# 66 narrow matmuls of ones in front, a bank of their own for the first state sums, and one routing step behind the last gate sums

## The chip, the core and the metric

The kernel runs on one core of one Trainium2 chip. The metric is device time in microseconds (us) of one execution; lower is better.

## The reference

A gated linear recurrence (4 batches, 8 heads, 768 steps, 48 channels a head) feeds a mixture of experts with two levels of routing (3072 tokens of 384 channels, 4 groups of 4 experts, 1024 hidden units). Cut to what matters:

```python
f = 1.0 / (1.0 + np.exp(-f_logit))
for t in range(S):
    state = f[:, :, t, :, None] * state + np.einsum('bhd,bhe->bhde', k[:, :, t], v[:, :, t])
    y[:, :, t] = np.einsum('bhd,bhde->bhe', q[:, :, t], state)
x = y.transpose(0, 2, 1, 3).reshape(B * S, H * D)
# each token: best group by x @ w_group, best expert in it by x @ w_expert[g]
h = np.maximum(x_of_expert @ w1[g, e], 0.0)
out[tokens] = (g_weight * e_weight)[:, None] * (h @ w2[g, e])
```

## The kernel before

**Two stages.** The first computes the recurrence in chunks of 128 steps and routes the tokens; the second gathers each expert's tokens and runs the two layers. The first stage is cut into 12 units: unit i is chunk c = i // 2 and the batch pair s = i % 2. Each unit goes through steps that have one-letter names: `c` bounds the gate logits (L597, VectorE); `g` takes Exp and Ln of them (L607, L610, ScalarE), sums the logarithms along time by a matmul with a triangle (`cs`, L616, TensorE) and takes Exp of the sums both ways (`eq` L617, `kh` L618); `m` multiplies q and k by them (L636, L639, VectorE); `t` turns both by TensorE transposes (`tr_q`, `tr_k`, L650) that ScalarE copies out (L651); `s` makes the scores (`ap`, L704 or L689) and masks them on VectorE (`am`, L707 or L692); `n` makes the chunk's state sums (`ds`, L721, TensorE) and on VectorE the next state (`st`, L726 to L729); `w` makes the outputs (`y`, L741 to L753), copied to `xT` by ScalarE (L756); `d` and `x` make the routing logits (`lT`, `lg`, L769, L774) and the rows of x (`x_ps`, L794) that are written to `x_dram`; `b` brings the chunk's decays (L659).

**Routing.** When both units of a chunk are done, a routing generator (`route`, L188) stands in a queue, and each step `r` takes it one yield further. For each chunk it ranks the tokens, writes weights and token numbers as `meta` into `x_dram` (L256, issued by GpSimd), and multiplies one-hot matrices `ln` and `val` (made by VectorE, L236, L243) into the slot table (`tb`, L261, TensorE; added by VectorE, L266). After the fourth chunk (`CLOSE`, c = 3) the two smallest experts are chosen, and GpSimd gathers their rows from `x_dram` (`xg`, L404). Those are turned on TensorE (`xg_ps`, L440) by step `e`, and their layers fill TensorE while the last routing runs.

**What sets the order.** TensorE, VectorE, ScalarE and SyncE run in exactly the order in which the program issues the work (`manual_schedule`, L85). That order is written by hand as strings of step names: `BEGIN` (L844) for the first three units, then `EVEN`, `ODD` or an entry of `ORDERS` (L850) for each later i; a name's number is the unit, in the later strings relative to i. GpSimd's order is left to the scheduler. In `BEGIN` the two steps `n0 n1` stand next to each other: the second step of unit 0 (VectorE makes its state, L729) and the first of unit 1 (TensorE makes its sums).

**PSUM.** Of the eight banks, seven belong to a pool from which `bank()` (L80) takes one for each product, the one that has been free longest. The eighth is the tile `ds` (L534), which holds the state sums of every unit. A tile whose reader has not finished makes the next writer wait; the program's semaphores see to that.

**The start.** SyncE issues the loads of the first units. Ahead of all other matmuls TensorE runs ten matmuls of ones in bf16 (`warm`, L892 to L894) whose product nobody reads: 128 rows, 128 weight columns, 512 columns that pass through. They wait only for VectorE's memset of `onesb` (L107).

Of the kernel before, what the change touches and what calls it, by code (L numbers as in the profile page):

```python
# [10 lines left out]
FP32 = mybir.dt.float32  # L11
# [7 lines left out]
P = 128  # L19
# [4 lines left out]
def kernel(  # L24
# [12 lines left out]
    nc = tc.nc  # L37
    B, H, S, D = q.shape
# [7 lines left out]
    HP = H // 2  # L46
    DP = 64
# [29 lines left out]
    def const(shape, dtype, name):  # L77
        return cp.tile(shape, dtype, tag=name, name=name)

    def bank(shape, name):  # L80
        return ps.tile(shape, FP32, tag="bank", name=name)
# [11 lines left out]
    onesb = const([P, P], BF16, "onesb")  # L93
# [305 lines left out]
    def fetch(pool, rows, n, top=N, late=False):  # L399

        w = {"n": n, "pool": pool, "early": top < N, "late": late, "blocks": [(j, min(P, n - j * P)) for j in range((n + P - 1) // P)]}
        w["x"] = pool.tile([P, len(w["blocks"]), RW], FP32, tag="xg", bufs=2 if pool is ep else 6, name="xg")
        for j, m in w["blocks"]:
            nc.gpsimd.indirect_dma_start(out=w["x"][:, j, :], out_offset=None, in_=x_dram[0:1 + top, :], in_offset=bass.IndirectOffsetOnAxis(ap=rows[:, j:j + 1], axis=0))  # L404
        return w
# [124 lines left out]
    with ExitStack() as fast:  # L530
        sb = fast.enter_context(tc.tile_pool(name="sb", bufs=2))
        fp = fast.enter_context(tc.tile_pool(name="fp", bufs=1))
        sums = fast.enter_context(tc.tile_pool(name="sums", bufs=1, space=bass.MemoryType.PSUM))
        ds = sums.tile([P, 2, HP, D], FP32, tag="ds", name="ds")  # L534

        def kept(shape, name):
            return fp.tile(shape, FP32, tag=name, name=name)
# [24 lines left out]
        NU = len(units)  # L562
# [21 lines left out]
        def load(i, names):  # L584
            c, s = units[i]
            w = live.setdefault(i, {"v": pads["v"][i % 4], "qh": pads["qh"][i % 3]})
            for nm in names:
                if nm not in w:
                    w[nm] = sb.tile([P, 2, H, D], FP32, tag="ld_" + nm, bufs=3 if nm == "f" else 2, name="ld_" + nm)
                for b in parts(i) if nm == "f" else (slice(0, 2),):  # L590
                    nc.sync.dma_start(out=heads(w[nm][:, b])[:, :, 0:D], in_=SRC[nm][2 * s + b.start:2 * s + b.stop, :, c * P:(c + 1) * P, :].rearrange("b h t d -> t (b h) d"))
# [118 lines left out]
        def stated(i):  # L710

            c, s = units[i]
            w = live[i]
            if c == NC - 1:
                return
            old, new = states[s][c % 2], states[s][(c + 1) % 2]
            wide = D if i else DP
            for a in range(HP):
                for b in range(2):
                    for r in range(2):  # L720
                        nc.tensor.matmul(ds[DP * r:DP * r + wide, b, a, :], lhsT=w["kh"][:, b, 2 * a + r, 0:wide], rhs=w["v"][:, b, 2 * a + r, 0:D], start=True, stop=True)  # L721
            yield
            dst = new[:, :, :, 0:D]
            gv = w["g"].unsqueeze(3).broadcast_to((P, 2, HP, D))
            if c:
                nc.vector.tensor_tensor(dst, old[:, :, :, 0:D], ds, OP.add)  # L726
                nc.vector.tensor_tensor(dst, dst, gv, OP.mult)
            else:
                nc.vector.tensor_tensor(dst, ds, gv, OP.mult)  # L729
            yield  # L730
# [103 lines left out]
        def advance(gens):  # L834
# [6 lines left out]


        STAGES = {"c": bounded, "g": gated, "m": multiplied, "t": turned, "z": crossed, "s": scored, "n": stated, "w": weighed, "d": done, "x": listed, "b": decayed}
        BEGIN = """c0 g0 p g0 g0 m0 m0 m0 m0 l2 t0 t0 t0 t0 h c1 g1 g1 s0 s0 s0 s0 g1 g1 p w0 w0 n0 m1 m1 m1 m1 l3 h x0 x0 x0  # L844
            t1 t1 t1 t1 b1 c2 g2 g2 s1 s1 s1 s1 p d0 g2 g2 n0 n1 w1 w1 m2 m2 l4 n1
# [4 lines left out]
        ORDERS = {  # L850
            NU - 4: "l+2 o d-2 n-1 r r r x-1 x-1 t t t t g+1 g+1 x-1 r z s s w s s c+2 d-1 g+2 w g+2 n m+1 m+1".split(),
            NU - 3: "l+2 o d-2 r r x-1 x-1 t t t t b n-1 r g+1 g+1 x-1 r s s s s c+2 w d-1 g+2 w g+2 n m+1 m+1 r n".split(),
            NU - 2: "d-2 r x-1 x-1 r t t t t r g+1 g+1 x-1 s s s s w d-1 w n m+1 m+1 k".split(),
            NU - 1: "d-2 r r n-1 x-1 x-1 t t t t r x-1 r s s s s w b d-1 w r r".split(),
            NU: "d-2 r e d-1 x-1 x-1 d-1 x-1 r r r e e r e r r e r r e r e r r e e e e e".split(),
        }
# [32 lines left out]
        load(1, ("qh", "k"))  # L889
        load(2, ("f",))  # L890
        load(1, ("v",))
        warm = bank([P, 4, P], "warm")  # L892
        for _ in range(10):
            nc.tensor.matmul(warm, lhsT=onesb, rhs=onesb.unsqueeze(1).broadcast_to((P, 4, P)), start=True, stop=True)  # L894
        for tok in BEGIN:
            step(tok[0], int(tok[1:] or 0))
        for i in range(BEGUN, NU + 1):
# [67 lines left out]
    for n in range(GE - 1):  # L965
        w = ws[n]
# [105 lines left out]
    with tc.If(more > 0), ExitStack() as late:  # L1072
# [5 lines left out]
        with tc.For_i(0, last, 1) as i:  # L1078
# [14 lines left out]
            w = fetch(ep, row, P, late=True)  # L1093
# [32 lines left out]
```

## Time and profile before

| | |
|---|---|
| time, median of 3 runs | 420.16 us (418.62 to 420.23) |
| the profiled execution's own time | 416.59 us |
| its span, first to last instruction | 414.8 us |
| TensorE: matmuls / weight loads, busy share | 97% / 89% |
| VectorE, ScalarE, GpSimd, busy share | 64%, 39%, 20% |
| HBM traffic over the span | 213 GB/s |
| first stage, about | 0 to 136 us |
| second stage, about | 136 us to the end |

How to read the views. In the timeline a line gives the start in us, the duration in us, the engine, the line of the program, the operation, output and input, partitions and elements, the count, and in brackets how long the engine had been idle and what ended that. PE is TensorE's matmuls, PEld its weight loads, which overlap them; DVE is VectorE, ACT ScalarE, POOL GpSimd, SP SyncE; a q behind a name is the engine's queue of DMA issues. A matmul's duration includes its way through the array, so consecutive matmuls overlap in the records: the distance between two starts says how long one occupies TensorE. fp32 matmuls are recorded as two each. In the list of waits a line names who waited, for whom, the total in us, how often, and the longest. TensorE's own idle time is short beside its busy time; an engine that isn't the bottleneck can be idle at no cost.

### The profile page before, as it was taken

What the parts mean: (1) busy time and instruction counts of PE and PEld (TensorE: products, weight loads), DVE (VectorE), ACT (ScalarE), POOL (GpSimd) and SP (SyncE); (2) the same over time, 40 slices, a digit from 0 to 9 for tenths busy, and PEclk for the clock granted to TensorE, in tenths of its full rate; (3) what the DMA queues carried; (4) which work ended last, traced back from release to release, by engine and by line L of the source; (5) the groups of instructions that cost most, each with busy time, mean ns of one, the idle gap of its engine ahead of it and who ended that gap; (6) DMA issues with size and microseconds to landing.
All of it is one profiled execution on the core that took longest, in us unless ns stands there. A gap on an engine that the chain in (4) does not pass through costs nothing.

```text
span 414.8 us, 10271 instructions
## 1 busy us (share of the span) xinstructions
PE 403.0 (97%) x4143; PEld 371.1 (89%) x4143; DVE 264.6 (64%) x780; ACT 162.7 (39%) x365; POOL 84.4 (20%) x132
## 2 busy tenths in 40 slices
PE   8989999999999999999999999999999999999994
PEld 3878878888878978989999999999999999999992
DVE  6666787778898722630899768486595595584230
ACT  6767878788555412211213122222232232232220
POOL 5000010101012157001042221311311230120230
PEclk9999999999999999999999999999999999999999
DMA  9999886869999459974829468586496596585010
GB/s 191 200 223 206 174 162 135 159 139 263 262 358 346 148 184 338 394 273 180 292 70 334 149 231 275 156 314 224 156 350 184 203 344 198 185 318 163 28 47 24
DMA packets 132146, 88.99 MB, mean 215 GB/s; under 512 B 102582, under 2 KB 122748, under 8 KB 132090
## 3 DMA queue, kind: packets, MB, share of 16 engines
q1 hardware_dynamic: 125666, 75.50, 61.2%
q0 software_dynamic: 5792, 11.92, 9.5%
q10 hardware_dynamic: 632, 0.83, 0.6%
q8 instruction: 35, 0.57, 0.5%
q14 instruction: 21, 0.17, 0.1%
HBM read 78.71 MB, written 9.83 MB: 213 GB/s over the span
## 4 chain that ended last, share of the span: by engine, by line
PE 47%; issue 30%; DMA 8%; POOL 6%; DVE 5%; ACT 2%; POOLq 1%; DVEq 0%
PE hp L450 12%; DMA out_dram<-yt,xg 7%; PE yo L486 7%; PE yo L471 4%; POOL out_dram L461 4%; PE cs L616 3%; POOL xg L404 2%; PE y L753 2%; PE ap L689 2%; PE x_ps L794 2%; PE tr_k L650 2%; DMA xg<-x_dram,rows_e 2%; PE tr_q L650 2%; PE y L745 2%; PE y L741 2%
## 5 line engine op out<-in xcount | busy, mean ns | idle before, releaser
L450 PE MATMUL hp<-xe,w 128*128 128x128 f32 (+14 forms) x864 | 138.6, 320 | 0.0
L450 PEld LDWEIGHTS hp<-xe,w 128*128 128x128 f32 x864 | 135.8, 190 | 0.8
L486 PE MATMUL yo<-h,w 128*128 128x230 f32 (+13 forms) x672 | 115.8, 333 | 0.0
L433 DVE STREAM_TRANSPOSE yr<-yT 32x192 f32<-32x192 f32 (+1 forms) x208 | 70.5, 339 | 70.4 <-ACT yT L487 67.8
L486 PEld LDWEIGHTS yo<-h,w 128*128 128x128 f32 x672 | 113.7, 190 | 0.2
L426 DVE STREAM_TRANSPOSE xe<-xg 32x192 f32<-32x192 f32 (+1 forms) x208 | 69.7, 335 | 8.6 <-PE hp L450 5.6
L451 ACT ACTIVATE h<-hp 128x256 f32<-128x256 f32 (+14 forms) x72 | 34.4, 478 | 103.5 <-PE hp L450 103.5
L461 POOL DMA_INDIRECT out_dram<-yt,xg x32 | 34.5, 1078 | 148.1 <-ACT yt L458 142.5
L487 ACT COPY yT<-yo 128x230 f32<-128x230 f32 (+13 forms) x42 | 13.5, 326 | 80.5 <-PE yo L486 80.5
L404 POOL DMA_INDIRECT xg<-x_dram,rows_p x30 | 29.6, 987 | 53.7 <-DMA out_dram<-yt,xg 25.4
L471 PE MATMUL yo<-w,h 128*128 128x384 f32 x64 | 21.3, 486 | 0.0
L707 DVE TENSOR_TENSOR am<-ap,tri 128x512 f32<-128x512 f32 x24 | 14.9, 681 | 8.5 <-PE ap L704 8.5
L616 PE MATMUL cs<-ld_f,tri 128*128 128x384 f32 x48 | 19.0, 521 | 0.0
L471 PEld LDWEIGHTS yo<-w,h 128*128 128x128 f32 x64 | 11.9, 190 | 7.4
L623 POOL DMA_DIRECT2D ends<-eq x10 | 5.4, 541 | 55.0 <-ACT eq L617 55.0
L458 ACT ACTIVATE yt<-yr,xg 128x384 f32<-128x384 f32 (+13 forms) x26 | 14.4, 604 | 5.4 <-DVE yr L433 5.4
L756 ACT COPY xT<-y 128x512 f32<-128x512 f32 x24 | 13.4, 587 | 7.5 <-PE y L745 5.4
L692 DVE TENSOR_TENSOR am<-ap,seen 128x384 f32<-128x384 f32 x24 | 12.2, 552 | 5.8 <-PE ap L689 5.8
L650 PE MATMUL tr_q<-ident,qh 128*128 128x128 f32 x96 | 14.5, 273 | 0.7 <-issue 0.6
L651 ACT COPY Tk<-tr_k 128x512 f32<-128x512 f32 x24 | 15.0, 629 | 0.0
L651 ACT COPY Tq<-tr_q 128x512 f32<-128x512 f32 x24 | 14.8, 618 | 0.4 <-PE tr_q L650 0.4
L617 ACT ACTIVATE eq<-cs 128x384 f32<-128x384 f32 x24 | 12.4, 518 | 5.2 <-PE cs L616 5.0
(187 smaller groups left out, 438.0 us busy)
## 6 DMA issues: line engine op xcount, KB each, us to landing
w<-in_moe_w_dram SPq DMA_DIRECT2D x34, 1536.0 KB, 8.4
qh<-in_q_dram SPq DMA_DIRECT2D x12, 384.0 KB, 4.7
ld_k<-in_k_dram SPq DMA_DIRECT2D x12, 384.0 KB, 4.0
v<-in_v_dram SPq DMA_DIRECT2D x12, 384.0 KB, 5.5
ld_f<-in_f_logit_dram SPq DMA_DIRECT2D x11, 384.0 KB, 5.5
x_dram<-x_kept SPq DMA_DIRECT2D x2, 1536.0 KB, 9.4
x_dram<-x POOLq DMA_DIRECT2D x2, 384.0 KB, 7.1
x_dram<-x ACTq DMA_DIRECT2D x2, 384.0 KB, 6.1
```

What stands on the lines that cost most here:

```text
L404: nc.gpsimd.indirect_dma_start(out=w["x"][:, j, :], out_offset=None, in_=x_dram[0:1 + top, :], in_offset=bass.IndirectOffsetOnAxis(ap=rows ...
L426: squares(w, lambda n, k_, rk, g, rg: nc.vector.transpose(out=xT[rg, 0:n, k_], in_=x[rk, 0:n, g]))
L433: squares(w, lambda n, k_, rk, g, rg: nc.vector.transpose(out=y[rk, 0:n, g], in_=yT[rg, 0:n, k_]))
L450: nc.tensor.matmul(hp[:, o, :], lhsT=w1[:, ko, (f + o) * P:(f + o + 1) * P], rhs=w["xT"][:, ko, :], start=(ko == 0), stop=(ko == KO - 1))
L451: nc.scalar.activation(h[:, f:f + 2, :], hp, AF.Relu)
L461: sent = nc.gpsimd.indirect_dma_start(out=out, out_offset=bass.IndirectOffsetOnAxis(ap=w["x"][0:m, j, DM + 1:RW].bitcast(U32), axis=0), in ...
L471: nc.tensor.matmul(yp, lhsT=w["h"][:, fo, :], rhs=w2[:, fo, :], start=(fo == 0), stop=(fo == FO - 1))
L486: nc.tensor.matmul(yp, lhsT=w2[:, fo, m * P:(m + 1) * P], rhs=w["h"][:, fo, :], start=(fo == 0), stop=(fo == FO - 1))
L616: nc.tensor.matmul(cs.rearrange("t h d -> t (h d)"), lhsT=tri, rhs=nl[:, b], start=True, stop=True)
L650: nc.tensor.transpose(out=pt[:, a, :], in_=w[nm + "h"][:, b, 2 * a:2 * a + 2, :].rearrange("t r d -> t (r d)"), identity=ident)
L651: nc.scalar.copy(w["T" + nm][:, b], pt)
L707: nc.vector.tensor_tensor(am[:, r], ap[r], tri.unsqueeze(1).broadcast_to((P, HP, P)), OP.mult)
```

## The change

Three edits. The warm-up becomes 66 matmuls of 128 columns in place of ten of 512. The state sums of unit 0 go to a bank of the pool, and the tile of the eighth bank (now called `later`) holds those of the units after it; units 0 and 1 (not only unit 0) use 64 weight columns a head, so that the whole of either bank is written. In the string for i = 10 (`NU - 2`) one `r` moves from ahead of `g+1 g+1` to behind it: on TensorE the `tb` matmuls of the fourth chunk follow the `cs` matmuls of unit 11 instead of going ahead of them.

```diff
-        ds = sums.tile([P, 2, HP, D], FP32, tag="ds", name="ds")
+        later = sums.tile([P, 2, HP, D], FP32, tag="ds", name="ds")
...
             old, new = states[s][c % 2], states[s][(c + 1) % 2]
-            wide = D if i else DP
+            wide = D if i > 1 else DP
+            ds = later if i else bank([P, 2, HP, D], "ds")
             for a in range(HP):
...
-            NU - 2: "d-2 r x-1 x-1 r t t t t r g+1 g+1 x-1 s s s s w d-1 w n m+1 m+1 k".split(),
+            NU - 2: "d-2 r x-1 x-1 r t t t t g+1 g+1 r x-1 s s s s w d-1 w n m+1 m+1 k".split(),
...
-        warm = bank([P, 4, P], "warm")
-        for _ in range(10):
-            nc.tensor.matmul(warm, lhsT=onesb, rhs=onesb.unsqueeze(1).broadcast_to((P, 4, P)), start=True, stop=True)
+        warm = bank([P, 1, P], "warm")
+        for _ in range(66):
+            nc.tensor.matmul(warm, lhsT=onesb, rhs=onesb.unsqueeze(1).broadcast_to((P, 1, P)), start=True, stop=True)
```

The orders of VectorE, ScalarE, GpSimd and SyncE are the same in both programs; on TensorE the order differs only in these places. From unit 0's sums on, the pool hands out its banks in another rotation.

## The prediction

> **What bounds the kernel now.** I read the page first, then TensorE's waits, then the timeline of the three places that the change touches, then who waits for what follows them. TensorE (PE) sets the pace:
>
> ```profile
> PE 403.0 (97%) x4143; PEld 371.1 (89%) x4143; DVE 264.6 (64%) x780; ACT 162.7 (39%) x365; POOL 84.4 (20%) x132
> ...
> PEclk9999999999999999999999999999999999999999
> ```
>
> PE is busy almost throughout, so a stall taken out of its queue should come off the end, unless a later stall takes it back. The waits of PE are few; four of them matter here (engine, line, what it waited for, total us, times, longest):
>
> ```profile
> PE ds L721 <- DVE st L729: 1.2, 1, 1.2
> PE warm L894 <- DVE onesb L107: 1.0, 1, 1.0
> PE tb L261 <- DVE val L243: 0.8, 1, 0.8
> PE xg_ps L440 <- DMA xg<-x_dram,rows_e: 0.7, 1, 0.7
> ```
>
> The change touches the first three. The fourth comes after all of them, and will matter. The timeline of the start (start us, us):
>
> ```profile
> 1.04 4.45 PE L894 MATMUL warm<-onesb 128*128 128x512 bf16 x10 [1.04 <-DVE onesb L107]
> ...
> 5.35 2.25 PE L616 MATMUL cs<-ld_f,tri 128*128 128x384 f32 x4
> ...
> 5.84 0.52 ACT L610 ACTIVATE ld_f<-ld_f 128x384 f32<-128x384 f32 x1
> ...
> 6.99 0.49 ACT L617 ACTIVATE eq<-cs 128x384 f32<-128x384 f32 x1 [0.62 <-PE cs L616]
> ...
> 8.75 1.02 DVE L639 SCALAR_TENSOR_TENSOR kh<-kh,ld_k 128x384 f32<-128x384 f32 x2
> ...
> 11.44 1.98 PE L704 MATMUL ap<-Tq,Tk 48*64 48x128 f32 x64
> ```
>
> The ten warm matmuls end just as the first sums (cs) can begin. Behind cs lies a chain without slack: eq on ACT, the products qh and kh on DVE back to back until 9.77, the turning of kh and the gates on PE, then ap. What moves cs moves all of it. The line of cs gives min/median/max ns:
>
> ```profile
> L616 PE MATMUL cs<-ld_f,tri x48: 486/486/979, 5.3 to 118.6; 128*128 128x384 f32 x48
> ```
>
> The 979 ns is the very first, at 5.35; the fourth, at 7.11, takes 486. The first two records occupy PE from 5.35 to 6.76 (0.70 each), the third from 6.76 to 7.11 (0.36). So PE ran at half speed until about 6.76, although the PEclk row shows nines from the start: that row can't be used here. The warm loads fit: their starts are 0.425 us apart for 512 columns, 0.106 per 128.
>
> **What the Trainium skill says.** "TensorE: Matmul & The Clock Gate", Part 1: a cold TensorE runs at half clock and is released after a sustained busy window of about 3.4 us, and the window is free-running, so the moment varies between executions. The trace agrees as far as it goes: PE began at 1.04 and was released near 6.76, 5.7 us later, between one window and two. The same page, "Back-to-back issue gap": 128 columns cost N/1.2 ns cold (107; the trace's 106) and N/2.4 + 2.5 ns warm (56; no row shows bf16 at 128 columns warm). "PSUM — Partial Sum Buffer", section on bank collisions: a writer and a reader of one bank must be kept apart by semaphores. That is the ds wait of 1.2 us: PE may not write unit 1's state sums while DVE has yet to read unit 0's from the same bank.
>
> **Part 1, 66 warm matmuls of 128 columns.** Removed: 10 x 0.425 = 4.25 us of PE. Added: 66, at 0.106 until the release and about 0.055 after. With the release at 6.76: (6.76 - 1.04) / 0.106 = 54 cold ones, and 12 x 0.055 = 0.66, end 7.42. cs then starts at 7.42 instead of 5.35, but warm: its first result is there at 7.42 + 0.36 + 0.49 = 8.27 instead of 6.95, +1.3 us for the whole chain. The release is free-running, so I bound it. At 4.45 (one window after 1.04): 32 cold, 34 x 0.055, end 6.3, first cs at 7.2. The old kernel, released then too, would gain 0.4 against its profile (ACT's second Ln ends at 6.36 and DVE's memsets at 7.33, so not more): the difference is 0.2 + 0.4 = +0.6. At 7.86 (two windows): end 8.0, first cs 8.8, +1.9; the old one then runs its second cs cold too and loses 0.7; difference +1.2. So +0.6 to +1.3; I take **+1.0**. No cover hides it: the old warm-up ended where its input arrived (Ln of the first half ends at 5.24), the new one outlasts that by 1 to 2.7 us.
>
> **Part 2, another bank for unit 0's state sums.** PE and then DVE, from their timelines around it:
>
> ```profile
> 23.06 1.56 PE L616 MATMUL cs<-ld_f,tri 128*128 128x384 f32 x4
> 25.82 0.93 PE L721 MATMUL ds<-v,kh 128*48 128x48 f32 x32 [1.20 <-DVE st L729]
> 26.57 1.93 PE L745 MATMUL y<-am,v 128*64 128x128 f32 x32
> ```
>
> ```profile
> 25.21 0.55 DVE L729 TENSOR_TENSOR st<-ds,decays 128x384 f32<-128x384 f32 x1
> ```
>
> The sums of unit 1 wait for DVE's L729 at 25.21, which stands behind masks and constants in DVE's order. With a bank of their own they start when cs has left PE: 23.06 + 4 x 0.33 = 24.4 instead of 25.82, -1.4. Their inputs are old (kh from 17.7), and y behind them needs am, which DVE ends at 24.20. What is late next: the second xT copy on ACT, then x_ps and tr_q at about 28.2 instead of 29.68; qh is ready at 26.63, kh at 27.50, in time. The borrowed bank is held from 16.6 to 25.8, leaving six in the ring; I followed the new bank waits of the built program up to unit 2, and each is on a reader that ends before PE gets there (tr_k on gw copies, done 18.4; second cs on am, done 22.4). The 64 wide weights cost nothing: 16 matmuls of 48 columns, as before. Between 0 (if the ring bites) and -1.5; I take **-1.4**. The steps up to 98.9 us are a chain of PE work, so it is carried on; from there DVE and ACT lead, but started by PE's ap.
>
> **Part 3, tb behind the last cs.** PE:
>
> ```profile
> 117.43 0.29 PE L261 MATMUL tb<-val,ln 128*128 128x64 bf16 x4 [0.85 <-DVE val L243]
> 117.55 1.54 PE L616 MATMUL cs<-ld_f,tri 128*128 128x384 f32 x4
> 119.02 2.06 PE L704 MATMUL ap<-Tq,Tk 48*128 48x128 f32 x32
> ```
>
> cs needs only Ln of unit 11, done at 114.86, so it can run from 116.45, when tr_k leaves PE, to 117.9; val is ready at 117.37, so tb then waits for nothing, and ap starts at 118.05 instead of 119.02: -0.95 on PE. Behind tb in its new place is only ap. DVE reads tb at 118.62; tb's result is there at 118.2. DVE's, ACT's, POOL's and SP's orders don't change, nor any DMA's place. But PE's next stall, on POOL's chain, then PE's:
>
> ```profile
> 119.25 0.76 POOL L256 DMA_DIRECT2D x_dram<-meta  x1 [2.36 <-DVE number L304]
> 126.35 1.07 POOL L404 DMA_INDIRECT xg<-x_dram,rows_e  x1 [6.33 <-DVE best L204]
> ```
>
> ```profile
> 133.37 0.33 PE L774 MATMUL lg<-ident,lgT 128*128 128x128 f32 x1
> 134.38 0.52 PE L440 MATMUL xg_ps<-ident,xg 128*128 128x128 f32 x3 [0.68 <-DMA xg<-x_dram,rows_e]
> ```
>
> PE stands before xg_ps until the gather lands. The gather follows the meta write (issued 119.25, landing 6.2 us later), and that follows DVE's own queue, busy without a gap from 106 to 120. None of it comes earlier because PE does. So PE arrives 0.95 sooner and waits 0.95 longer. Bounds: 0 to -0.95; I take **-0.2**, for small things such as x rows sent earlier. Parts 1 and 2 are not swallowed so: they shift DVE's queue too.
>
> **Sum.** 1.0 - 1.4 - 0.2 = -0.6 on the profiled execution's 416.59 (span 414.8 and 1.8 around it): 416.0. The three timed runs have a median of 420.16, 3.6 above it; the same step on the median gives **419.6 us**.
>
> **Rivals.**
> (B) The timed runs lack the early release. They lie 2.0 and 3.6 us above the profiled one; one window late costs half of 3.4, 1.7, and two cost 3.4. If the input arrives late in them, PE has a gap between the warm matmuls and cs and the window fails. 66 cold matmuls last 7.0 us, over two windows, so they always contain a whole one. Then the new kernel runs as the good profile did, 416.0 plus up to 1: 416.8. For it: the steps of 2.0 and 1.6. Against: a gather of 7.9 us under weight loads can vary as much.
> (C) Slower: the loads of the warm matmuls don't hide. A cold load is 0.15 us in the trace; if a pair took 0.15 + 0.106 = 0.256, 22 would be done at 6.76 and the other 44 take 5.6, end 12.4, +6.3 for cs: 6.3 - 1.6 = +4.7, 424.9. In general the end is at 3.9 + 33 x the cold pair's time; from 0.115 us the gains are eaten, from 0.18 it is slower by over 0.5%. Against: tb's four pairs of 64 columns start 0.03 us apart, so loads hide there.
> (D) The ds gain doesn't reach the end (a ring or DMA wait before 98.9): 420.16 + 1.0 = 421.2.
>
> **Chances.** A (forecast) 0.47, 418.5 to 420.6; B 0.31; D 0.14; C 0.08. A measurement of this kernel can tell about 0.5%, 2.1 us, from no change. Faster by more: B and a little of A, 0.34. Slower by more: C and the top of D, 0.11. Same: 0.55. The range runs from inside B to the top of D, 416.4 to 421.7.
>
> **What would show it.** Right: the first cs record at 486 ns and starting 1 to 2.7 us later; no ds wait; no tb wait, and the xg_ps wait grown from 0.7 to about 1.6. Wrong: cs before 6.3 or after 8.1; timed runs near the profiled one (B); the ds gain missing at tr_q of unit 2; an xg_ps wait that doesn't grow.

## The result, and the profile after

The changed kernel takes 418.36 us (median of 19 runs, 417.51 to 420.36); the old one, run beside it on the same chip, 420.19 (19 runs, 417.97 to 421.29). The medians are 1.8 us apart; the ratio of all the runs is 0.9965, 95% interval 0.9950 to 0.9979: 1.5 us or 0.35% less, between 0.9 and 2.1 us. The 1.5 is used below. The profiled execution took 417.55 us (span 415.7). This is 1 us above the one of before (416.59), although the timed runs are faster. The stretch from 158 to 168 us, below, answers how that can be.

The page of the changed kernel, its busy times and the granted clock:

```profile
PE 405.3 (97%) x4199; PEld 376.0 (90%) x4199; DVE 263.9 (63%) x780; ACT 162.3 (39%) x365; POOL 84.4 (20%) x132
...
PEclk9999999999999998999999999999999999999998
```

There are 56 more matmuls; the other counts are the same. New in the clock row are the 8 in the slice from 156 to 166 us and the one in the last slice; only the first of them matters here. The waits of PE (total us, times, longest):

```profile
PE hp L450 <- issue: 2.0, 3, 0.9
PE warm L895 <- DVE onesb L107: 1.0, 1, 1.0
...
PE y L754 <- issue: 0.3, 1, 0.3
```

The waits of ds and tb are gone, as the edits meant, and so is that of xg_ps. The first line is new, and it is the largest. "Issue" means that nothing the profile shows held PE up.

The start (start us, us):

```profile
1.05 5.14 PE L895 MATMUL warm<-onesb 128*128 128x128 bf16 x66 [1.05 <-DVE onesb L107]
...
6.02 1.51 PE L616 MATMUL cs<-ld_f,tri 128*128 128x384 f32 x4
...
6.92 0.49 ACT L617 ACTIVATE eq<-cs 128x384 f32<-128x384 f32 x1 [0.55 <-PE cs L616]
```

cs starts 0.67 us later than before and runs at full speed (1.51 us for the four records, 2.25 before), so that eq starts at 6.92, even 0.07 earlier than the 6.99 of before. In this one execution the long front cost nothing. PE at unit 1 and what follows it:

```profile
22.99 1.56 PE L616 MATMUL cs<-ld_f,tri 128*128 128x384 f32 x4
24.48 1.14 PE L722 MATMUL ds<-v,kh 128*64 128x48 f32 x32
25.45 1.93 PE L746 MATMUL y<-am,v 128*64 128x128 f32 x32
...
28.56 0.60 PE L650 MATMUL tr_q<-ident,qh 128*128 128x128 f32 x4
```

From cs to tr_q of unit 2 it is 5.57 us, where it was 6.62: 1.05 less. Note ds: it starts 1.49 after cs, and y 0.97 after ds, where the old kernel with its 48 weight columns in that place had 0.75. Then the end of the first stage:

```profile
113.77 1.46 PE L616 MATMUL cs<-ld_f,tri 128*128 128x384 f32 x4
115.06 0.28 PE L261 MATMUL tb<-val,ln 128*128 128x64 bf16 x4
115.27 2.06 PE L704 MATMUL ap<-Tq,Tk 48*128 48x128 f32 x32
...
130.03 0.52 PE L440 MATMUL xg_ps<-ident,xg 128*128 128x128 f32 x3
```

xg_ps, the first work of the second stage, starts at 130.03, 4.35 us earlier than the 134.38 of before. Yet the span is 0.9 longer. From xg_ps to the end it is 285.7 us, where it was 280.4. These 5.3 us are lost in one place, between 158 and 168 us:

```profile
160.34 0.51 PE L450 MATMUL hp<-xe,w 128*128 128x128 f32 x3 [0.64 <-issue]
...
161.74 0.27 PE L450 MATMUL hp<-xe,w 128*128 128x128 f32 x1 [0.90 <-issue]
...
163.20 0.96 ACT L451 ACTIVATE h<-hp 128x256 f32<-128x256 f32 x3 [4.42 <-remote]
163.25 0.94 DVE L441 COPY xe<-xg_ps 128x384 f32<-128x384 f32 x2 [9.69 <-remote]
```

PE, ACT and DVE stand still together, and ACT and DVE go on within 0.05 us of each other. "Remote" says that the profile knows no releaser on this core. Right after it the granted clock falls (start and end of the stretch; the last three numbers are clock, DMA share and GB/s):

```profile
160.00:165.00 5.00, 2.67 (x12) 1.99 (x12) 1.73 (x5) 0.96 (x3) 1.22 (x2) 0.92 1.01 357
165.00:170.00 5.00, 5.00 (x21) 4.63 (x20) 4.63 (x14) 0.56 (x1) 0.00 (x0) 0.74 1.04 402
```

The profile of before, on which the prediction rests, has no such stall: there ACT, DVE and PE run through. The two profiles therefore don't compare in their spans, and I set out to separate the three edits, the stall and the chip. From here on "the stall" is this stop of all three engines, and a "pause" is a wait of PE alone that the profile calls issue.

### The profile page after: what moved, and what is told of

Its sections match the earlier page's. It is cut to its first block, busy times and chain, and to the rows that moved or that the text cites. A ratio compares the mean times of both kernels' runs of the same rounds, so it can differ in the third digit from the quotient of the medians.

```text
span 415.7 us, 10379 instructions
## 1 busy us (share of the span) xinstructions
PE 405.3 (97%) x4199; PEld 376.0 (90%) x4199; DVE 263.9 (63%) x780; ACT 162.3 (39%) x365; POOL 84.4 (20%) x132
## 4 chain that ended last, share of the span: by engine, by line
PE 51%; issue 30%; DMA 6%; POOL 6%; DVE 2%; ACT 2%; POOLq 1%; another core or an unknown queue 1%; ACTq 0%
PE hp L450 12%; PE yo L486 6%; DMA out_dram<-yt,xg 6%; PE yo L471 4%; POOL out_dram L461 4%; PE cs L616 4%; PE y L754 3%; PE y L746 3%; PE x_ps L795 2%; POOL xg L404 2%; PE ap L704 2%; PE tr_k L650 2%; PE tr_q L650 2%; PE ap L689 2%; PE y L742 2%
## 5 line engine op out<-in xcount | busy, mean ns | idle before, releaser
L450 PE MATMUL hp<-xe,w 128*128 128x128 f32 (+14 forms) x864 | 141.3, 323 | 2.6 <-issue 2.0
L450 PEld LDWEIGHTS hp<-xe,w 128*128 128x128 f32 x864 | 137.5, 192 | 4.4 <-issue 2.4
L441 DVE COPY xe<-xg_ps 128x384 f32<-128x384 f32 (+1 forms) x4 | 2.1, 535 | 20.6 <-PE xg_ps L440 10.9
```

The source lines that it names most:

```text
L450: nc.tensor.matmul(hp[:, o, :], lhsT=w1[:, ko, (f + o) * P:(f + o + 1) * P], rhs=w["xT"][:, ko, :], start=(ko == 0), stop=(ko == KO - 1))
```

## The experiments

Twelve runs on four chips; the kernels of one group ran on one chip beside the same runs of the old kernel: group p on one (old kernel 420.66 us), group q on a second (420.20), s on a third (415.23), t on a fourth (415.26). A ratio is always to the old kernel on the same chip.

**p0, the old kernel again.** No edit.

> The old kernel once more, for a second profile and a clock for each run. Theory A (dependencies alone): the profile looks as the first, span near 414.8 us plus or minus 1, cs records cold until about 5 to 8 us, no PE wait at 160 us. Theory B (late clock release in most runs): the cs and tr records at 5 to 12 us are cold (979 ns for cs, over 400 ns for tr), first ap later than 12.5 us, and the time is 2 to 4 us above the first profile. Theory S (stalls that no dependency explains, at places where PE, ACT and DVE all stand still under a full DMA, as the new kernel has at 158 to 163 us): the start is as in the first profile, but a stall of 2 to 5 us shows near 160 us, with cold matmuls behind it and a mean clock near 0.993 rather than 0.998.

Measured: 419.99 us against 420.66, ratio 0.9995 (0.9977 to 1.0013). This is what theory S expected. The profiled execution has a span of 420.5 instead of 414.8, and the stall at 162 to 167 us (ACT 4.46 and DVE 9.66 idle, "remote"; clock 0.67 and 0.65 from 165 to 175). So the stall belongs to the old kernel as well, and the profile of before was one without it.

**p1, the front alone.**

```diff
-        warm = bank([P, 4, P], "warm")
-        for _ in range(10):
...
+        warm = bank([P, 1, P], "warm")
+        for _ in range(66):
...
```

> Only the 66 narrow warm matmuls. Theory A: slower than the old kernel by 0.6 to 1.3 us (cs later by 1 to 2 us but warm); 0 if the release comes early as in the new kernel's profile. Theory B: faster by 1.5 to 3.5 us, nearly all that the whole change brings. Theory S: the 112 additional instructions on PE's queue move where the unexplained stalls of 0.6 to 1 us inside the y matmuls fall, so the time between the cs of unit 3 and of unit 9 is shorter by 1 to 2 us, and the sum is about -1 us.

Measured: 422.47 us, ratio 1.0035 (1.0009 to 1.0061; 6 runs): slower, as theory A had it, by 1.5 us plus or minus 1.1. The start of its profile:

```profile
1.05 6.41 PE L894 MATMUL warm<-onesb 128*128 128x128 bf16 x66 [1.05 <-DVE onesb L107]
...
7.29 1.51 PE L616 MATMUL cs<-ld_f,tri 128*128 128x384 f32 x4
```

Unit 1's cs is 1.43 later than in p0, and the delay stays so up to unit 4. Then it changes with PE's pauses (0.7 us in all here, 1.5 in p0): it is 2.1 at unit 5, 0.7 at unit 9 and 0.98 at the last lT but one. The rest goes at the next step, where p0 waits for the gather and p1 does not. p0's line is

```profile
133.83 0.52 PE L440 MATMUL xg_ps<-ident,xg 128*128 128x128 f32 x3 [0.66 <-DMA xg<-x_dram,rows_e]
```

and in p1 xg_ps starts at 134.00 without a wait, only 0.17 later. So the gather, which the prediction let take back the third edit alone, took back more than half of the first one's delay in this profile.

**p2, the bank alone.**

```diff
-        ds = sums.tile([P, 2, HP, D], FP32, tag="ds", name="ds")
+        later = sums.tile([P, 2, HP, D], FP32, tag="ds", name="ds")
...
-            wide = D if i else DP
+            wide = D if i > 1 else DP
+            ds = later if i else bank([P, 2, HP, D], "ds")
```

> Only the bank of unit 0's state sums. Theory A: the ds wait of 1.2 us goes, tr_q of unit 2 at about 28.6 us instead of 29.7, the time falls by 1.0 to 1.4 us. Theory B: the same, beside the spread. Theory S: the gain of 1.1 us at tr_q of unit 2 shows, but the end moves by anything from 0 to -1.4, because a stall near 160 us can take it back.

Measured: 418.80 us, ratio 0.9964 (0.9944 to 0.9984; 20 runs): 1.5 us less, as much as the whole change brings. Its profile:

```profile
23.08 1.56 PE L616 MATMUL cs<-ld_f,tri 128*128 128x384 f32 x4
24.57 1.14 PE L722 MATMUL ds<-v,kh 128*64 128x48 f32 x32
...
28.65 0.60 PE L650 MATMUL tr_q<-ident,qh 128*128 128x128 f32 x4
```

From cs to tr_q it is 5.57, in p0 6.63: 1.06 is gained. At xg_ps it is 1.5.

**p3, the moved tb alone.**

```diff
-            NU - 2: "d-2 r x-1 x-1 r t t t t r g+1 g+1 x-1 s s s s w d-1 w n m+1 m+1 k".split(),
+            NU - 2: "d-2 r x-1 x-1 r t t t t g+1 g+1 r x-1 s s s s w d-1 w n m+1 m+1 k".split(),
```

> Only tb behind the last cs. Theory A: ap after the last cs about 1.0 us earlier relative to the tr_k before it, and PE's wait for the gather before xg_ps longer by the same, so the time falls by 0 to 0.3 us. If the wait does not grow: the time falls by up to 1.0 us. Theory S: any gain up to 160 us can be taken back there, 0.

Measured: 420.78 us, ratio 0.9997 (0.9982 to 1.0011). Against p0 unit 11's cs is 1.32 earlier, the last lT but one 0.67 and the last 0.31. So 0.6 goes on the way, in PE's queue, and 0.4 stays in front of xg_ps, where p0 waited 0.7:

```profile
PE xg_ps L440 <- DMA xg<-x_dram,rows_e: 1.0, 1, 1.0
```

**q1, the second and third edits without the first.** The diff of p2 and that of p3.

> The changed kernel with its first edit undone: ten warm matmuls of 512 columns again, the bank for unit 0's sums and the moved tb kept. Theory A (dependencies): the front costs about 1 us and the bank brings 1.4, so this is the changed kernel less 1: about 417.5 us, ratio to the old kernel 0.994; the first cs starts at 5.3 to 5.5 and tr_q of unit 2 at about 28.4. Theory S (a stall of all engines between 155 and 170 us takes most differences of the first stage back or doubles them, whatever they are): the time stands with the length of that stall and not with the start, so this lies with the changed kernel within 0.3 us, 418.4 to 418.8.

Measured: 418.49 us, ratio 0.9960 (0.9942 to 0.9977). Its last lT is at 130.62, 3.7 earlier than p0's, and it too has the stall (ACT 3.78, DVE 9.86). The time lies where theory S put it (418.4 to 418.8); 1 us faster than the changed kernel, as theory A had it, is not seen: its ratio of 0.994 is just outside the interval.

**q2, the changed kernel with 66 warm matmuls of 77 columns.**

```diff
-        warm = bank([P, 1, P], "warm")
+        warm = bank([P, 77], "warm")
...
-            nc.tensor.matmul(warm, lhsT=onesb, rhs=onesb.unsqueeze(1).broadcast_to((P, 1, P)), start=True, stop=True)
+            nc.tensor.matmul(warm, lhsT=onesb, rhs=onesb[:, 0:77], start=True, stop=True)
```

> The changed kernel with 66 warm matmuls of 77 columns in place of 128: the same instructions, but as many columns in all (5082) as the old front's 5120. Theory A: the front costs nothing then, so the time is that of the kernel with the second and third edits alone, about 417.5 us (0.994); if a matmul can't start more often than every 0.07 us cold, it costs 0.3 more. Theory I (it matters how many instructions precede the rest): as the changed kernel, 418.4, and the pauses named issue inside y L753 are as few as there.

Measured: 418.03 us, ratio 0.9945 (0.9925 to 0.9966). 66 of 77 columns take 4.07 us (most of them 0.065 apart, the last eleven 0.035), less than the 4.45 of the ten of 512, and eq starts at 6.28. So at these widths the columns cost, and the number of matmuls does not. The time lies between the two expectations and decides nothing.

**q3, the old kernel with 66 of 77.** The same edit on the old kernel.

> The old kernel with 66 warm matmuls of 77 columns and nothing else: the number of instructions of the changed kernel's front, the length of the old one's. Theory A: same as the old kernel, ratio 1.000 within 0.001, about 420.2. Theory I (56 more instructions shift where the supply of instructions runs into y, so that the pauses named issue inside y L753 go): PE y L753 issue 0.3 instead of 1.0 to 1.4, and the last lT about 1 us earlier against unit 1's cs; time 419 to 419.5, ratio 0.998.

Measured: 420.69 us, ratio 1.0006 (0.9991 to 1.0020), as theory A had it. The pauses in y L753 fall to 0.4, but 0.9 appear in y L745; all pauses together are 1.5 as in p0, and the last lT but one is where it was.

**q4, the old kernel with 16 of 512 and one of 256.**

```diff
-        for _ in range(10):
+        for _ in range(16):
...
+        nc.tensor.matmul(warm[:, 0:2], lhsT=onesb, rhs=onesb.unsqueeze(1).broadcast_to((P, 2, P)), start=True, stop=True)
```

> The old kernel with 16 warm matmuls of 512 columns and one of 256: the columns of the changed kernel's front (8448) in few instructions. Theory A: the first cs starts 1 to 2.7 us later, unit 1 about 1.4 later as with 66 narrow ones, and the time is 421.2 to 421.6, ratio 1.0025 to 1.0035. Theory I: the pauses inside y L753 stay (1.0 or more), so the delay of 1.4 us is still there at the last lT, where 66 narrow ones had only 0.1 left of it.

Measured: 421.16 us, ratio 1.0016 (0.9998 to 1.0034). cs starts at 6.90, unit 1 is 1.0 late against p0, and at the last lT nothing of it is left in this profile (0.14 earlier), although there are only 7 matmuls more. Theory I, by which the pauses stay when few instructions are added, falls: they shrink here too (0.4 in all). In time, theory A's 1.0025 lies inside the interval, and so does no change.

**s1, fewer gathers ahead.** On q1's kernel:

```diff
-        w["x"] = pool.tile([P, len(w["blocks"]), RW], FP32, tag="xg", bufs=2 if pool is ep else 6, name="xg")
+        w["x"] = pool.tile([P, len(w["blocks"]), RW], FP32, tag="xg", bufs=2 if pool is ep else 3, name="xg")
```

> The kernel with the second and third edits, and three buffers for gathered rows in place of six: before the stall at 158 to 165 us GpSimd issues 5 gathers and not 11, so half of the small packets that share the DMA engines with the weights are gone from it. Theory G (the gathers behind a full DMA cause the stall): ACT's second h and DVE's xe come within 1 us of PE's products as in the first profile of the old kernel, no clock below 0.9 follows, and the time falls by 2 to 4 us to 414.5 to 416.5. Theory W (the weights alone fill the DMA, or the stall is of PE's power or clock): the stall of 4 to 5 us stays and the time is that of the second and third edits, 418.2 to 418.8.

Measured: 597.32 us, ratio 1.44: a miss of another kind. With three buffers the gather of pass n + 3 has to wait until pass n has sent its rows (the second line), and DVE, which turns the gathered rows, waits 228 us for gathers in all (the first; busy us, mean ns | idle before, and what ended most of it):

```profile
L426 DVE STREAM_TRANSPOSE xe<-xg 32x192 f32<-32x192 f32 (+1 forms) x208 | 69.7, 335 | 233.0 <-DMA xg<-x_dram,rows_p 228.4
...
L404 POOL DMA_INDIRECT xg<-x_dram,rows_p x30 | 29.2, 972 | 67.5 <-DMA out_dram<-yt,xg 47.0
```

The stall is absent, which would speak for theory G, were the old kernel not at 415.23 us on this chip (11 runs, mean clocks from 0.996 to 1.0, 0.989 to 0.997 on the two before). So the old kernel probably has no stall here either.

**s2, passes 2 and 3 without loads of their own.** On q1's kernel:

```diff
-            ahead[2] = load_weights(wp, who[0:1, PLACES[2]:PLACES[2] + 1])
+            ahead[2], kept_w = ahead[1], ahead[0]
...
-            ahead[n + 3] = load_weights(wq if n % 3 == 1 else wp, who[0:1, PLACES[n + 3]:PLACES[n + 3] + 1])
+            ahead[n + 3] = kept_w if n == 0 else load_weights(wq if n % 3 == 1 else wp, who[0:1, PLACES[n + 3]:PLACES[n + 3] + 1])
```

> The kernel with the second and third edits, but passes 2 and 3 use the weights of passes 1 and 0 over again: four loads of 1.5 MB are left out and the outputs of those passes are not the reference's; later loads come late, so only the stretch up to 185 us is compared. Theory W1 (DMA full of weights causes the stall): DMA share from 155 to 170 us falls to a third or less, the idle times of 4.4 us on ACT and 9.7 us on DVE up to 163 us and PE's pauses of 0.7 us go. Theory P (the stall is PE's own, of its power or clock): all of it stays though the DMA is empty.

Measured: one run, 412.91 us, of a kernel that leaves out loads its outputs need; DMA share 0.00 from 165 to 175 us, and no stall. On the same chip s1, at a share above 1 from 155 to 170, has none either, so this run can't decide between W1 and P.

**t1 and t2, the changed kernel and q1's kernel on a chip where the old one takes 415.26.** No edit, and that of q1.

> The changed kernel again, beside the kernel without its first edit, on whichever chip it is. Three chips have run the old kernel so far: at 420.7 and 420.2 us with a mean clock of 0.993, and at 415.2 with 0.998 to 1.0. Theory A (the forecast's dependencies): 0.6 us less than the old kernel on any chip, ratio 0.9985. Theory L (the 3.7 to 4.4 us by which the last lT comes earlier all reach the end where no stall at 158 to 168 us takes them back): on a chip where the old kernel takes 415, ratio 0.990 to 0.991; on one where it takes 420, 0.9965 as before.

> The second and third edits with the old front, on the same chip. Theory A: 1.0 us less than the changed kernel, ratio to it 0.9976, because nothing hides the longer front. Theory F (the front's delay is lost in pauses of PE further on): the same as the changed kernel within 0.3 us.

Measured: t1 413.74 us, ratio 0.9964 (0.9949 to 0.9978); t2 413.21 us, ratio 0.9957 (0.9941 to 0.9972). Theory L falls, theory A's 0.6 lies outside t1's interval, and the ratio is that of the other chip. Between t1 and t2 it is 0.3 us in the mean, plus or minus 0.8, which fits theory F and doesn't quite exclude A's 1.0. The two profiles side by side do not show a loss on the way: t1's cs is 1.70 behind t2's at unit 1, its xg_ps 1.30, its span 1.4 longer. The same lines as above, here in t1:

```profile
158.48 0.39 ACT L451 ACTIVATE h<-hp 128x256 f32<-128x256 f32 x1 [0.88 <-PE hp L450]
...
160.02 0.94 DVE L441 COPY xe<-xg_ps 128x384 f32<-128x384 f32 x2 [4.33 <-PE xg_ps L440]
...
160.08 12.19 PE L450 MATMUL hp<-xe,w 128*128 128x128 f32 x72
```

ACT and DVE are released by PE, and PE goes through 72 matmuls without a gap, at the same DMA share (1.02 to 1.03 from 155 to 175 us). So this profile can be set beside that of before, which also lacks the stall. The start of each unit's cs, that of xg_ps, and the span, in us:

| | unit 1 | unit 3 | unit 6 | unit 9 | unit 10 | unit 11 | xg_ps | span |
|---|---|---|---|---|---|---|---|---|
| before | 13.35 | 34.34 | 63.30 | 94.93 | 105.32 | 117.55 | 134.38 | 414.8 |
| t1 | 14.64 | 34.59 | 62.60 | 92.88 | 104.36 | 115.56 | 132.16 | 412.6 |
| difference | +1.29 | +0.25 | -0.70 | -2.05 | -0.96 | -1.99 | -2.22 | -2.2 |

Read from left to right: the front costs 1.29; the bank gives 1.04 (unit 3); from there to unit 9 t1 gains 2.3, most of it because PE paused in before (1.6 us) and not here; in unit 10 t1 has a pause of its own (0.81) and loses 1.1; the moved tb gives 1.0; and what is left at xg_ps, 2.22, is in the span to the tenth. In this pair of executions the second stage passes the gain on whole; over the timed runs the gain is 1.5. Such pauses look like this, two in before and one in t1:

```profile
58.61 0.27 PE L753 MATMUL y<-am,other 128*48 128x64 f32 x2 [0.78 <-issue]
...
80.41 0.25 PE L753 MATMUL y<-am,other 64*48 64x64 f32 x1 [0.60 <-issue]
...
99.31 0.26 PE L754 MATMUL y<-am,other 128*48 128x64 f32 x1 [0.81 <-issue]
```

They fall in the middle of a run of matmuls of one line, whose inputs have been there all along. The traces show more. From 10 to 138 us the fourteen profiles have 21 pauses of 0.2 us or more. Count PE's matmuls from the start of the program: all 21 stand at seven places, numbers 852 to 854, 978, 1232 to 1233, 1486, 1739, 1993 to 1995 and 2371, which are about 127 apart or a multiple of that. They stand there with the old front and the new one, although the 56 additional matmuls put other work there: number 1993 is in ds in p0 and in y in p1. And each pause ended 1.2 to 1.6 us after a packet of 16 KB had landed from this queue of the page (packets, MB, share; here t1):

```profile
q8 instruction: 35, 0.57, 0.5%
```

Between two of its packets PE begins about 250 matmuls and weight loads, which are 125 pairs. So at these places PE, it seems, waits for its next block of instructions. An edit that adds or removes instructions moves other work to these places. Most blocks arrive in time (some 20 packets and at most three pauses in each profile); what makes one late was not tried.

## Why the prediction was right or wrong

**The base.** The prediction carried its step from the profile of 416.59 to the median of 420.16 without an explanation for the 3.6 us between them, and rival B explained them by a late clock release at the start. B is refuted. Eight profiles with the old front of ten matmuls have the first eq between 6.40 and 7.13, a spread of 0.7 us and no more. What differs is the stall at 158 to 168 us. It is in all nine profiles taken on chips where the old kernel takes about 420, and in none of the four taken where it takes 415, nor in the profile of before. On which chip that one was taken is not on record: its 416.59 is below every timed run of the old kernel on the slower chips (417.97 and more), and its mean clock of 0.998 above theirs (0.997 at most). It may come from the other kind, whose slowest run took 416.31. From xg_ps to the end of the span it is 280.4 us in t1 and 280.3 in t2, as in before. The timed runs agree: on the two slower chips the old kernel's runs with a mean clock of 0.996 to 0.997 average 419.1 us, those at 0.992 to 0.994 420.3, those at 0.989 to 0.991 421.6. Carrying the step over was right all the same: the ratio is 0.9965 on one kind of chip and 0.9964 on the other.

**Part 1, +1.0.** The mechanism and its size at the start are right. With the release at 6.76 the prediction put the end of the warm matmuls at 7.42; p1 and t1 have cs at 7.29 and 7.38. The changed kernel's first profile has it at 6.02, earlier than the 6.3 that I had called the earliest and a sign of being wrong. Over all profiles the first eq is at 7.80 on average with 66 x 128 (8.19, 6.92, 8.28) and at 6.74 with the ten (eight profiles): +1.06.

What did not hold in full is "no cover hides it". Two things can cover the delay. One is the gather: the prediction said that parts 1 and 2 are not swallowed there, but p1's delay fell from 0.98 to 0.17 at that wait. The other is pauses of PE, which stood in the waits of before as "issue" and were put at nothing: q4's delay of 1.0 was gone where PE paused 0.4 us in place of p0's 1.5. In t1 against t2 nearly all of it stayed. In time, four pairs of kernels differ in the front's length alone, with ratios apart by 0.0035 (p1), 0.0016 (q4), 0.0005 (changed kernel and q1) and 0.0007 (t1 and t2). Weighted by their intervals that is 0.6 us, plus or minus 0.5, so that the 1.0 lies at the edge. On the old kernel the front costs about what was forecast: sorted into the three classes of clock above, the runs give 1.3 (p1) and 1.1 (q4), plus or minus 0.6 and 0.4, an estimate that takes it that the edit does not choose the class. In company with the other edits it is 0.2 to 0.3, plus or minus 0.9. Why it should cost less there is not shown.

As to the clock: "TensorE: Matmul & The Clock Gate", Part 1, of the Trainium skill, gives a busy window of about 3.4 us, free-running. The spread of the release fits, its lower end does not. Single warm matmuls show the release: they start 0.107 us apart before it and 0.056 after it, and it came 2.7 us after the first matmul in the first profile, 5.4 in p1 and 5.5 in t1. So the page's 3.4 was no lower bound here.

**Part 2, -1.4.** The mechanism is right: ds waits for nothing and starts when cs has left PE. The size at tr_q of unit 2 is 1.05 in all these profiles. Two terms were off. cs holds PE for 1.49 and not for 1.34 (23.06 to the 24.4 of the prediction, which had itself read 0.36 for one record at the start and then took 0.33), and "the 64 wide weights cost nothing" is wrong: from ds to y it is 0.97 instead of 0.75. 1.4 - 0.15 - 0.22 = 1.03. "TensorE: Matmul & The Clock Gate", section "LDWEIGHTS (loading the stationary operand)", could have told me: a load takes its columns / 1.2 in ns, so 16 columns more cost 13 ns each, and 16 matmuls 0.21 us, as an estimate. The records agree: two matmuls follow each other by 45 ns with 48 weight columns and by 59 with 64, 0.22 us for the sixteen. I had counted only what passes through. That the widths do it was read from the records and not tried by itself. In the time the bank brought 1.5 us (p2, between 0.7 and 2.4). That this is so near the forecast's 1.4 is luck: 1.05 of it is explained, and the other 0.4 is within the interval or comes from pauses (0.7 us in p2, 1.5 in p0) and the stall.

**Part 3, -0.2.** PE gains what was foreseen: from the last tr_k before it to ap it is 1.94 us instead of 3.04. In the time the edit alone gives 0.0003, 0.1 us, plus or minus 0.6. But "none of it comes earlier because PE does" is only half true. Alone (p3), PE waited longer for the gather, as said (1.0 in place of 0.7, not the 1.6 I gave). In company there is no such rule: PE does not wait at all in the changed kernel and 0.4 us in t1, which is the same program, and 0.3 in q1, 0.9 in t2, 1.0 in s1 and 1.6 in s2, whose first stages are the same. A wait that does not grow was another sign named for being wrong. From the issue of meta to that of the gather it takes 7.1 us in before and p0, 8.2 in p2, 7.8 in p3 and in s2, and 6.2 to 6.7 in the changed kernel, q1, t1 and t2. So the stretch is not a constant that stands behind DVE; it varies by 2 us, and with it the wait that I had taken for a fixed wall. What it depends on was not tried.

**The sum.** Forecast -0.6, measured -1.5 on both chips (0.9965 and 0.9964), within 0.4 if the two are taken together. Edits two and three were put at -1.6 and measured at 1.7 to 1.8 less (q1 0.9960, t2 0.9957), plus or minus 0.7 each. So the missing 0.9 is most likely in the first term, in this company; alone that term was about right. The single edits, 1.5, -1.5 and -0.1 us, add up to -0.1 and not to the -1.5 of the whole, but their intervals are too wide to make anything of it. The 418.36 us lie 1.2 below the forecast. They are inside the whole range, and 0.35% is within the 0.5% that were forecast, but they are just below the band of A, 418.5 to 420.6: the range was wide enough to hold it because it reached into rival B, which is refuted. That is luck too.

**The rivals.** C is refuted: in t1 the narrow matmuls start 0.107 us apart while cold, and with 77 columns 0.065 (q2), so the weight loads hide. "TensorE: Matmul & The Clock Gate", section "Back-to-back issue gap", gives N/1.2 ns cold, 107 for 128 columns and 64 for 77, and the trace agrees. D is refuted by p2.

**What stays open.** First, the pauses. All together they are 1.6, 1.5 and 1.5 us in the three profiles of kernels with the old front and the old bank, 1.5 in q3, and 0 to 0.8 in the ten others. Where they can fall is seen, at the borders of PE's blocks of instructions; which of them come is not: before and p0, the same program, share only one of three places. Second, the stall: it is something else, since it stops three engines, comes in hp of the same pass in all kernels, and in p0 no packet of the instruction queue falls between 146.9 and 176.6 us, around it. Full DMA doesn't suffice for it (t1), and whether it needs it could not be tried, since both runs meant for that fell on a chip without it. Third, the chips: each was used in one session, so that chip and hour can't be told apart. The best version tried is the one without the longer front, 418.49 and 413.21 us, but nothing here tells it from the changed kernel.

## What to carry to other kernels

A warm-up that goes on after its successor's input has arrived delays the start by what its last matmuls take; size it by columns, not by the number of matmuls, and expect the release of the clock at a different time in each execution (2.7 to 5.5 us after the first matmul here). A wait in a chain of one engine is worth its length less what the cure adds, so cost the wider operands that the cure needs too. Before a step of 0.5% is carried from a profile to timed runs, see that both have the same stalls: two profiles of the old kernel differed by 5.7 us, four times what the whole change brings. And when a profile shows PE waiting for "issue" among ready matmuls, look at the packets of the instruction queue before a cause is sought in the data.

## What the runs showed of the hardware

- Chips can differ: the old kernel takes 420.7 and 420.2 us on two, 415.2 and 415.3 on two others, and the ratio of the changed kernel is the same on both kinds (0.9965 and 0.9964).
- On the slower kind PE, ACT and DVE can stall together with no releaser on the core (ACT for 3.8 to 4.5 us), while DMA is full; PE then issues small groups some 0.7 or 1.4 us apart, and in eight of nine such profiles the mean granted clock from 165 to 175 us is 0.66 to 0.92.
- PE's pauses of 0.2 to 0.9 us named "issue" stand, in the first stage, at fixed numbers in its program, about 127 matmuls apart or a multiple of that, and end 1.2 to 1.6 us after a 16 KB packet of the instruction queue (21 of 21, in twelve of fourteen profiles).
- The clock row of the page doesn't show the cold start: it has a nine where the matmuls run at half speed.
- A gather that must wait for an earlier pass to send its rows cost about 180 us (s1, 597.32 against the old kernel's 415.23): six buffers for rows are no luxury there.
